# Gate and value of a SwiGLU feed-forward as block products of four by four blocks, 26 for 28 Strassen products, on one Trainium2 core

## Chip, cores, metric

One core of a Trainium2 chip (trn2), fp32 throughout. The time is the device time of one execution in microseconds (us), lowest is best. Before: 3118.09 us, the median of 4 runs (3117.6 to 3118.33) beside the changed kernel.

Engines in the profile: PE is TensorE's matmuls, PEld its weight loads, DVE is VectorE, ACT ScalarE, POOL GpSimd, SP the engine that only issues transfers here. L516 is line 516 of the kernel that is named.

## What is computed

```python
def _attn_ref(x, filt_r, filt_i):          # x: 8 x 3008 x 256
    X = np.fft.rfft(x, axis=1)
    Y = X * (filt_r + 1j * filt_i)[None, :, :]
    return np.fft.irfft(Y, n=x.shape[1], axis=1).astype(np.float32)

def _moe_ref(x, w_gate, w_val, w_out):      # x: 24064 tokens x 256; d_ff = 1536
    g = x @ w_gate
    silu = g * (1.0 / (1.0 + np.exp(-g)))
    return (silu * (x @ w_val) @ w_out).astype(np.float32)
```

The Fourier part is done by matmuls too (pa, pb, pc, pd in the profile). For each of 8 batches the feed-forward runs over 4 chunks of 752 tokens, while TensorE also does the Fourier part of the next batch in between. So there are 32 chunks, and the stretch of one batch is four of them.

## The kernel before

Gate and value are each a 2 x 2 block Strassen product with 7 products of 376 columns, for 6 slices of d_ff: 84 products a chunk. Twice a chunk, after three slices, the hidden values are projected back, with 7 products again (63 matmul pairs of 128 columns each time).

```python
    def hidden(b, k, j, y, fill):
        ...
            nc.tensor.matmul(out=bk[z][kind], lhsT=wt[z][:, j, LEFT[p], :], rhs=y[:, RIGHT[p], :],
                             start=start, stop=True, skip_group_check=True)
        ...  # banks are evicted by ScalarE (copies to u) and VectorE (u + bank)
        e = nc.gpsimd                      # Strassen sums of the hidden block for the projection
        add(e, h[:, 4], h[:, 1], h[:, 2])
        sub(e, h[:, 5], h[:, 0], h[:, 1])
        sub(e, h[:, 1], h[:, 4], h[:, 0])
        sub(e, h[:, 6], h[:, 3], h[:, 1])

    def project(b, k, q):
        ...
        def place(i, cb, a, kind):
            dst = o[i][:, :, ts(cb, 128)]
            if q:                          # not the first projection of the chunk
                add(nc.gpsimd, dst, dst, u[a])
                add(nc.vector, dst, dst, bk[kind])
            else:
                add(nc.vector, dst, u[a], bk[kind])
        ...
        product(7, "A", False)
        nc.scalar.copy(out=u[2], in_=bk["A"])
        place(1, 1, 2, "E")                # reads bank E ...
        product(4, "F4")
        place(1, 0, 2, "F4")
        product(3, "E", False)             # ... and this adds onto bank E
        place(0, 1, 1, "E")
```

`place(1, 1, 2, "E")` must have read bank E before the last product may add onto it.

Of the kernel before, what the change touches and what calls it, by code (L numbers as in the profile page):

```python
# [55 lines left out]
NQB = 2  # L57
JB = NJ // NQB

# [5 lines left out]

LEFT = {1: 0, 2: 1, 7: 2, 4: 3, 5: 4, 6: 5, 3: 6}
RIGHT = {1: 0, 2: 1, 3: 2, 4: 3, 5: 4, 6: 5, 7: 6}
WO = {1: 0, 7: 1, 2: 2, 3: 3, 5: 4, 6: 5, 4: 6}
HID = {1: 0, 6: 1, 4: 2, 2: 3, 5: 4, 7: 5, 3: 6}

# [33 lines left out]
def kernel(  # L104
# [30 lines left out]
    ypool = pool("yp", 2)  # L135
    dpool = pool("dram", 2, DRAM)
    fps = pool("fps", 2, PSUM)
    wps = pool("wps", 2, PSUM)
# [3 lines left out]
    wg_t = cpool.tile([128, NJ, 7, 128], FP32)  # L142
    wv_t = cpool.tile([128, NJ, 7, 128], FP32)
# [25 lines left out]
    def weight_parts():  # L169

        cols = [w.bitcast(U32).rearrange("(a p) (h j f two) -> j p h a f two",
                                         a=2, p=128, h=2, j=NJ, two=2)
                for w in (moe_w_gate, moe_w_val)]
        rows = moe_w_out.bitcast(U32).rearrange("(l j p) (c f two) -> j p l c f two",
                                                l=2, j=NJ, p=128, c=2, two=2)
        def hid(j):
            for w, dst in zip(cols, (wg_t, wv_t)):
                yield w[j], dst[:, j], True

        for q in range(NQB):  # L180
            for j in range(JB * q, JB * q + JB):
                yield from hid(j)
            for j in range(JB * q, JB * q + JB):
                yield rows[j], wo_t[:, j], False

    weights = list(weight_parts())
    raws = {}

    def load_weights(j, queue=nc.sync):
        if j < len(weights):  # L190
            raws[j] = rpool.tile([128, 2, 2, 128, 2], U32, name=f"raw_{j}", tag="raw", bufs=2)
            for i in range(2):
                ins = queue.dma_start(out=raws[j][:, i], in_=weights[j][0][:, i])
                if j in (2, 3):
                    tc.keep_in_program_order(ins)

    def round_weights(j, following=True):



        if following:
            load_weights(j + 2)
        raw, (_, dst, left) = raws.pop(j), weights[j]
        low, high = raw[:, :, :, :, 0], raw[:, :, :, :, 1]
        pw = rpool.tile([128, 2, 2, 128], U32, name=f"pw_{j}", tag="pw")
        w = rpool.tile([128, 2, 2, 128], FP32, name=f"w_{j}", tag="w")
        man = w.bitcast(U32)
        v = nc.vector
        flat = "p a b f -> p (a b f)"
        flat2 = "p a b f two -> p (a b f) two"  # L210
# [7 lines left out]
        pin(nc.scalar.activation(out=pw, in_=pw, func=AF.Relu, bias=off_t))  # L218
        v.tensor_scalar(out=pw, in0=pw, scalar1=255.0, scalar2=2.0 ** 23,
# [6 lines left out]
                               op0=ALU.mult, op1=ALU.add)  # L226

        e = nc.gpsimd
        pin(e.tensor_tensor(out=dst[:, 0:4, :].rearrange("p (a b) f -> p a b f", b=2), in0=w,  # L229
                            in1=pw.bitcast(FP32), op=ALU.mult))  # L230
        if left:
            a11, a12, a21, a22, s1, s2, s4 = [dst[:, i] for i in range(7)]
            add(e, s1, a21, a22)
            sub(e, s2, s1, a11)
            sub(e, a21, a11, a21)
            sub(e, s4, a12, s2)
        else:
            b11, b12, b21, b22, t1, t2, t4 = [dst[:, i] for i in range(7)]
            sub(e, t1, b12, b11)
            sub(e, t2, b22, t1)  # L240
            sub(e, b12, b22, b12)
            sub(e, t4, b21, t2)
# [3 lines left out]
    def bank(kind, name):  # L246
        return wps.tile([128, 512], FP32, name=f"w{kind}_{name}", tag=kind)

    def warm(count, width=4):


        for i in range(count):
            ps = bank("F", "idle")[:, 0:128 * width]
            tc.keep_in_program_order(nc.tensor.matmul(
                out=ps, lhsT=wv_t[:, 0, 0, :],
                rhs=wv_t[:, 0, 0:width, :].rearrange("p i f -> p (i f)"), start=True, stop=True))

    class Spectral:
# [81 lines left out]
        def stage2a(self, u):  # L340
# [6 lines left out]
            if self.b:  # L347
                ps = fps.tile([128, NV, C], FP32, name=f"pb_{self.b}_{u}", tag="f")
                ppool, qpool = apool, bpool
            else:  # L350

                ps = bank("AEF"[u % 3], f"b_{u}").rearrange("p (i c) -> p i c", i=NV)
                ppool = apool if u % 3 == 2 else spool0
                qpool = bpool if u % 2 else spool0
# [32 lines left out]
        def stage3(self, k, step):  # L387

            if step == 0:
                self.y[k] = ypool.tile([128, 7, TH], FP32, name=f"y_{self.b}_{k}", tag="y")  # L390
            y = self.y[k]
# [8 lines left out]
            def turned(p):  # L400
                return y[:, RIGHT[p], :].rearrange("p (r n) -> p n r", n=NH)

            def block(p):
                return y[:, RIGHT[p], :]

            if step == 0:
                nc.scalar.copy(out=turned(1), in_=psv)
            elif step == 1:
                nc.scalar.copy(out=turned(3), in_=psv)
            elif step == 2:  # L410
                sub(nc.vector, turned(5), psv, turned(1))
                sub(nc.vector, turned(7), turned(3), psv)
                sub(nc.gpsimd, block(6), block(3), block(5))
            else:
                nc.scalar.copy(out=turned(2), in_=psv)
                sub(nc.gpsimd, block(4), block(2), block(6))
# [5 lines left out]
    def hidden(b, k, j, y, fill):  # L422

        name = f"{b}_{k}_{j}"
        s = spool.tile([128, 4, TH], FP32, name=f"s_{name}", tag="s")
        h = hpool.tile([128, 7, TH], FP32, name=f"h_{name}", tag="h")
        dst = {"g": s, "v": h}
        wt = {"g": wg_t, "v": wv_t}
        bk = {"g": {}, "v": {}}
        ut = {}  # L430

        def product(z, p, kind, start=True):
            if start:
                bk[z][kind] = bank(kind, f"{z}{p}_{name}")[:, 0:TH]
            nc.tensor.matmul(out=bk[z][kind], lhsT=wt[z][:, j, LEFT[p], :], rhs=y[:, RIGHT[p], :],  # L435
                             start=start, stop=True, skip_group_check=True)

        def step(z, p):
            if p == 1:
                ut[z] = upool.tile([128, 3, 384], FP32, name=f"u_{z}_{name}", tag="u")  # L440
            u = [ut[z][:, i, 0:TH] for i in range(3)]
            if p in (1, 6, 7):
                product(z, p, "A", p == 1)
                nc.scalar.copy(out=u[(1, 6, 7).index(p)], in_=bk[z]["A"])  # L444
                if p == 7:
                    add(nc.vector, dst[z][:, 2], u[2], bk[z]["E"])
            elif p == 5:
                product(z, p, "E")
            elif p == 2:
                product(z, p, "F")  # L450
                add(nc.vector, dst[z][:, 0], u[0], bk[z]["F"])
            elif p == 4:
                product(z, p, "A", False)
                if z == "g":
                    nc.scalar.activation(out=s[:, 3], in_=bk[z]["A"], func=AF.Silu)
                else:
                    nc.vector.tensor_tensor(out=h[:, 3], in0=s[:, 3], in1=bk[z]["A"], op=ALU.mult)  # L457
            else:
                product(z, p, "E", False)
                add(nc.vector, dst[z][:, 1], u[1], bk[z]["E"])  # L460
                if z == "g":
                    nc.scalar.activation(out=s[:, 0:3], in_=s[:, 0:3], func=AF.Silu)  # L462
                else:
                    nc.vector.tensor_tensor(out=h[:, 0:3], in0=s[:, 0:3], in1=h[:, 0:3],  # L464
                                            op=ALU.mult)

        for it in ("g1", "v1", "g5", "v5", "g6", "v6", "", "g2", "g7", "v7", "v2", "",
                   "g4", "v4", "g3", "v3"):
            if it:
                step(it[0], int(it[1]))  # L470
            else:
                fill()

        e = nc.gpsimd
        add(e, h[:, 4], h[:, 1], h[:, 2])
        sub(e, h[:, 5], h[:, 0], h[:, 1])
        sub(e, h[:, 1], h[:, 4], h[:, 0])
        sub(e, h[:, 6], h[:, 3], h[:, 1])
        hids[b, k, j] = h

    def project(b, k, q):

        hs = [hids.pop((b, k, JB * q + i)) for i in range(JB)]
# [9 lines left out]
        def product(p, kind, start=True):  # L493
            if start:
                bk[kind] = bank(kind[0], f"o{p}_{name}")[:, 0:384].rearrange(
# [30 lines left out]
        if q == NQB - 1:  # L526
# [11 lines left out]
    todo = list(range(len(weights)))  # L538
# [3 lines left out]
    x0 = [wo_f[0:NR, 0:8 * C], wo_f[0:NR, 8 * C:16 * C]]  # L542
# [119 lines left out]
```

## Time and profile before

| | before |
|---|---|
| time | 3118 us |
| TensorE busy, granted clock | 98%, 0.99 |
| VectorE, GpSimd busy | 47%, 45% |
| one steady batch (4 chunks) | 376.2 us |
| of it matmul work | 373.7 us |

The ends of matmuls are modelled, their starts are not; so I took the start-to-start spacing of every matmul record and looked up what it is when nothing waits: 112 ns for one of 94 or 128 columns, 216 for 256, 316 for 376, 429 for 512 (each fp32 product is two such instructions). The sum of these is "work". What a spacing has above it is "half clock" as far as the clock records show half speed there, and "wait" otherwise. Over the whole run before: 3013.6 work, 15.9 half clock, 78.9 waits. The profile's lines on this kernel stand in the prediction.

### The profile page before, as it was taken

The numbers are of one execution on the slowest core, as the hardware profiler recorded it, in microseconds if no ns is written. First come the engines' busy times: TensorE is split into PE (matmuls) and PEld (weight loads), VectorE is DVE, ScalarE is ACT, GpSimd is POOL, SyncE is SP. The second block draws the span as 40 slices with busy tenths as digits, with TensorE's granted clock in tenths as the row PEclk, the third lists the DMA queues.
The fourth block names the chain that finished last, engine by engine and source line by source line (L and its number), as shares of the span: only waits on it lengthen the run. The fifth ranks groups of instructions, "written<-read, shape, count | busy, mean of one in ns | idle before, by whom it ended". The sixth has DMA issues, their size and how long they took to land.

```text
span 3116.7 us, 41163 instructions
## 1 busy us (share of the span) xinstructions
PE 3056.4 (98%) x15560; PEld 2240.5 (72%) x15560; DVE 1476.5 (47%) x2348; ACT 1140.3 (37%) x2070; POOL 1405.8 (45%) x1622
## 2 busy tenths in 40 slices
PE   7789999999999999999999999999999999999999
PEld 4457777777767777767777777767777677777776
DVE  4664553354543554345543455434553444544443
ACT  0443333333343343343333333343333433333333
POOL 3574454444543444444543454434544344533343
PEclk8999999999999999999999999999999999999999
DMA  8432222222212222222222132121322222200000
GB/s 233 130 117 68 72 81 56 61 76 68 75 55 72 59 79 60 61 68 81 69 60 65 57 88 71 51 71 55 91 68 56 63 63 68 68 28 21 21 6 16
DMA packets 123634, 212.51 MB, mean 68 GB/s; under 512 B 23670, under 2 KB 69750, under 8 KB 122578
## 3 DMA queue, kind: packets, MB, share of 16 engines
q1 hardware_dynamic: 91692, 132.25, 14.8%
q0 software_dynamic: 24448, 68.71, 7.7%
q10 hardware_dynamic: 7296, 8.92, 1.1%
q8 instruction: 123, 2.02, 0.3%
q14 instruction: 75, 0.61, 0.1%
HBM read 134.81 MB, written 74.97 MB: 67 GB/s over the span
## 4 chain that ended last, share of the span: by engine, by line
PE 80%; POOL 7%; DVE 6%; issue 3%; DMA 2%; ACT 2%; SPq 0%; POOLq 0%; ACTq 0%; DVEq 0%
PE wA_v L435 15%; PE wA_g L435 15%; PE wA_o L499 7%; PE wE_v L435 7%; PE wE_g L435 7%; PE wE_o L499 7%; PE wF_o L499 4%; PE wF_g L435 4%; PE pd L396 3%; PE wF_v L435 3%; POOL o L162 3%; PE pa L332 3%; POOL h L165 3%; PE pc L376 2%; PE pb L356 2%
## 5 line engine op out<-in xcount | busy, mean ns | idle before, releaser
L435 PE MATMUL wA_v<-y,wv_t 128*128 128x376 f32 x1536 | 612.5, 480 | 7.3 <-ACT u_v L444 4.3
L435 PE MATMUL wA_g<-y,wg_t 128*128 128x376 f32 x1536 | 614.3, 481 | 4.4 <-POOL wg_t L229 3.5
L165 POOL TENSOR_TENSOR h<-h 128x376 f32<-128x376 f32 x576 | 566.9, 984 | 28.8
L162 POOL TENSOR_TENSOR h<-h 128x376 f32<-128x376 f32 x192 | 188.4, 981 | 701.2 <-PE wE_v L435 389.1
L444 ACT COPY u_g<-wA_g 128x376 f32<-128x376 f32 x576 | 269.5, 468 | 589.9 <-PE wA_g L435 587.6
L435 PEld LDWEIGHTS wA_v<-y,wv_t 128*128 128x128 f32 x1536 | 289.2, 190 | 204.0 <-DVE h L457 15.6
L499 PEld LDWEIGHTS wA_o<-wo_t,h 128*128 128x128 f32 x3456 | 406.3, 192 | 16.3
L499 PE MATMUL wA_o<-wo_t,h 128*128 128x128 f32 x3456 | 417.5, 275 | 0.0
L435 PEld LDWEIGHTS wA_g<-y,wg_t 128*128 128x128 f32 x1536 | 281.1, 190 | 172.3 <-issue 28.1
L462 ACT ACTIVATE s<-s 128x1128 f32<-128x1128 f32 x192 | 219.5, 1143 | 373.2 <-DVE s L162 373.2
L464 DVE TENSOR_TENSOR h<-s,h 128x1128 f32<-128x1128 f32 x192 | 257.1, 1339 | 124.0 <-ACT s L462 124.0
L435 PE MATMUL wE_g<-y,wg_t 128*128 128x376 f32 x768 | 307.1, 482 | 2.1 <-DVE s L162 2.1
L435 PE MATMUL wE_v<-y,wv_t 128*128 128x376 f32 x768 | 306.1, 480 | 1.8 <-DVE h L162 1.6
L444 ACT COPY u_v<-wA_v 128x376 f32<-128x376 f32 x576 | 272.2, 473 | 69.3 <-PE wA_v L435 65.2
L162 DVE TENSOR_TENSOR s<-u_g,wE_g 128x376 f32<-128x376 f32 x384 | 208.9, 544 | 176.2 <-ACT u_g L444 174.6
L162 DVE TENSOR_TENSOR s<-u_g,wF_g 128x376 f32<-128x376 f32 x192 | 104.4, 544 | 394.9 <-PE wF_g L435 369.3
L499 PE MATMUL wE_o<-wo_t,h 128*128 128x128 f32 x2304 | 281.6, 276 | 7.5 <-DVE o L162 7.5
L499 PE MATMUL wF_o<-wo_t,h 128*128 128x128 f32 x2304 | 278.5, 275 | 0.0
L499 PEld LDWEIGHTS wE_o<-wo_t,h 128*128 128x128 f32 x2304 | 267.4, 192 | 13.6 <-DVE o L162 13.6
L499 PEld LDWEIGHTS wF_o<-wo_t,h 128*128 128x128 f32 x2304 | 267.8, 192 | 0.3
L162 POOL TENSOR_TENSOR p<-p,q 128x512 f32<-128x512 f32 x96 | 121.6, 1266 | 226.4 <-DVE q L367 226.4
L162 DVE TENSOR_TENSOR h<-u_v,wE_v 128x376 f32<-128x376 f32 x384 | 208.9, 544 | 26.5 <-ACT u_v L444 5.1
(86 smaller groups left out, 3275.3 us busy)
## 6 DMA issues: line engine op xcount, KB each, us to landing
t<-d SPq DMA_DIRECT2D x192, 128.0 KB
t<-d SPq DMA_DIRECT2D x64, 384.0 KB
d<-t POOLq DMA_DIRECT2D x112, 192.0 KB, 2.5
tb<-de_tbl SPq DMA_DIRECT2D x84, 256.0 KB
d<-g POOLq DMA_DIRECT2D x168, 128.0 KB, 2.8
x<-in_x_dram SPq DMA_DIRECT2D x112, 160.0 KB
out_dram<-o POOLq DMA_DIRECT2D x128, 128.0 KB, 2.0
f<-in_filt_r_dram SPq DMA_DIRECT2D x168, 64.0 KB
```

The source lines that it names most:

```text
L162: eng.tensor_tensor(out=dst, in0=a, in1=b, op=ALU.add)
L165: eng.tensor_tensor(out=dst, in0=a, in1=b, op=ALU.subtract)
L332: nc.tensor.matmul(out=ps[0:NK], lhsT=wf_t, rhs=self.x.pop(u), start=True, stop=True)
L356: nc.tensor.matmul(out=ps[:, i, :], lhsT=self.tb[u][:, i, 0, :], rhs=t2[:, i, :], start=True, stop=True)
L376: nc.tensor.matmul(out=ps[:, i, :], lhsT=tb[:, i, 1, :], rhs=pt[:, i, :], start=True, stop=True)
L396: nc.tensor.matmul(out=psv[:, n, :], lhsT=self.t4[k, i][:, n, ts(cb, 128)], rhs=wi_t, start=True, stop=True)
L435: nc.tensor.matmul(out=bk[z][kind], lhsT=wt[z][:, j, LEFT[p], :], rhs=y[:, RIGHT[p], :], start=start, stop=True, skip_group_check=True)
L444: nc.scalar.copy(out=u[(1, 6, 7).index(p)], in_=bk[z]["A"])
L462: nc.scalar.activation(out=s[:, 0:3], in_=s[:, 0:3], func=AF.Silu)
L464: nc.vector.tensor_tensor(out=h[:, 0:3], in0=s[:, 0:3], in1=h[:, 0:3], op=ALU.mult)
L499: nc.tensor.matmul(out=bk[kind][:, t, :], lhsT=hs[i][:, HID[p], t0:t0 + 128], rhs=wo_t[:, JB * q + i, WO[p], :], start=start and t == 0 an ...
```

## The change

The intent is to take matmul work off TensorE. The left operand is cut into groups of four blocks of 128 rows (two slices of d_ff, three groups a chunk), the sequence into four columns of blocks of 188 tokens, and one group's 4 x 2 by 2 x 4 block product takes 26 products where Strassen takes 28 and the plain form 32. Gate and value share their sequence operands and a bank. In exchange there are more sums: of the weights (26 a group, built once, kept in DRAM and loaded again for every group), of the sequence (26 tiles in y_t, once a chunk) and of the products. The projection comes three times a chunk with 42 matmul pairs.

```diff
-NQB = 2
-JB = NJ // NQB
+NG = 3
+JB = NJ // NG
+TQ = TH // 2
+ORDER = ("Q0 Q1 P0 P1 A01 Q2 E01 P2 B01 A02 A12 Q3 E02 B02 P3 E12 B12 "
+         "A03 A13 A23 E03 B03 E13 B13 E23 B23").split()
...
-    wps = pool("wps", 2, PSUM)
+    wps = pool("wps", 6, PSUM)
...
+    def reload_weights(g, piece):
+        a, b, _ = PIECES[piece]
+        nc.sync.dma_start(out=wt_t[:, a:b], in_=w_dram[g, :, a:b])
...
+        def sums(i, j):
+            r = rpool2.tile([128, 3, 2, TQ], FP32, name=f"r{i}{j}_{name}", tag="r")
+            rt[i, j] = [r[:, e] for e in range(3)]
+            add(nc.gpsimd, rt[i, j][0], qp[i][0], qp[j][1])
+            add(nc.vector, rt[i, j][1], qp[j][0], qp[i][1])
...
+            elif kind == "A":
+                sums(i, j)
+                nc.scalar.copy(out=rt[i, j][2], in_=ps)
+                add(nc.gpsimd if j == 2 else nc.vector, rt[i, j][1], rt[i, j][1], rt[i, j][2])
+            elif kind == "B":
+                sub(nc.vector, place(i, j), ps, rt[i, j][0])
+            else:
+                sub(nc.vector, place(j, i), ps, rt[i, j][1])
+            if p in ("B13", "B23"):
+                h = hs[p == "B23"]
+                nc.scalar.activation(out=h[:, 4:8], in_=h[:, 4:8], func=AF.Silu)
+                nc.vector.tensor_tensor(out=h[:, 0:4], in0=h[:, 0:4], in1=h[:, 4:8], op=ALU.mult)
+                e = nc.gpsimd
+                add(e, h[:, 4], h[:, 1], h[:, 2])
+                ...                        # three more; eight a group
...
             hidden(b, k, g, fill, after)
+            if k < NCHUNK - 1 and g == NG - 1:
+                combine_sequence(cur.y[k + 1])
             if late is not None:
                 project(*late)
```

## The prediction

> **What bounds the kernel now.** I read the page's busy shares first, then the groups with each shape kept apart, then the timeline of two projections, then the chain of waits through one of them.
>
> ```profile
> PE 3056.4 (98%) x15560; PEld 2240.5 (72%) x15560; DVE 1476.5 (47%) x2348; ACT 1140.3 (37%) x2070; POOL 1405.8 (45%) x1622
> ```
>
> TensorE is busy 98%, every other compute engine under half. But the ends of matmuls are modelled, so I take their cost from start to start:
>
> ```profile
> 1510.69 2.17 PE L499 MATMUL wF_o<-wo_t,h 128*128 128x128 f32 x18
> 1512.70 2.17 PE L499 MATMUL wE_o<-wo_t,h 128*128 128x128 f32 x18
> 1514.71 0.80 PE L435 MATMUL wA_g<-y,wg_t 128*128 128x376 f32 x2
> 1515.34 0.79 PE L435 MATMUL wA_v<-y,wv_t 128*128 128x376 f32 x2
> 1515.97 0.80 PE L435 MATMUL wE_g<-y,wg_t 128*128 128x376 f32 x2
> ```
>
> Each fp32 product is two instructions. Nine products of 128 columns start 2.01 us apart: 0.223 us each. One of 376 columns takes 0.63. Weight loads are hidden in both. One chunk (376 tokens per half, all of d_ff) recurs every 94.05 us: the first projection of a chunk starts at 1124.45 and, four chunks later, at 1500.64. Of this 84 hidden products make 53.2 us (84 x 0.633), 126 projection products 28.1, the spectral work of the next batch 12. So it is truly TensorE-bound, except at one place, the second projection of a chunk:
>
> ```profile
> 2017.18 1.33 DVE L464 TENSOR_TENSOR h<-s,h 128x1128 f32<-128x1128 f32 x1 [0.58 <-ACT s L462]
> ...
> 2018.66 0.98 POOL L162 TENSOR_TENSOR h<-h 128x376 f32<-128x376 f32 x1 [3.73 <-DVE h L464]
> 2019.60 0.98 POOL L165 TENSOR_TENSOR h<-h 128x376 f32<-128x376 f32 x1
> ...
> 2020.53 1.00 POOL L162 TENSOR_TENSOR o<-o,u 128x384 f32<-128x384 f32 x1
> 2021.49 2.04 POOL L165 TENSOR_TENSOR h<-h 128x376 f32<-128x376 f32 x2
> ...
> 2026.66 1.95 POOL L162 TENSOR_TENSOR o<-o,u 128x384 f32<-128x384 f32 x2 [2.18 <-ACT u L520]
> 2027.68 0.56 DVE L162 TENSOR_TENSOR o<-o,wE_o 128x384 f32<-128x384 f32 x1 [2.97 <-POOL o L162]
> ...
> 2028.29 1.94 PE L499 MATMUL wE_o<-wo_t,h 128*128 128x128 f32 x15 [0.22 <-DVE o L162]
> ```
>
> Here the last projection product adds onto a bank that VectorE must first read; VectorE first needs GpSimd's add into o; and GpSimd works off, in order, the sums of the hidden block that has just ended. TensorE waits 0.4 us only. This chain decides my prediction.
>
> **What the Trainium skill says.** "SBUF — State Buffer", Who interferes with whom: a VectorE operation with two SBUF inputs and a GpSimd operation that reads SBUF exclude each other for the whole instruction; with one input in PSUM there is no conflict. The trace agrees:
>
> ```profile
> L365 DVE SCALAR_TENSOR_TENSOR q<-pb,f 64x512 f32<-64x512 f32 x84 | 58.2, 693 | 1.1
> ...
> L224 DVE SCALAR_TENSOR_TENSOR w<-raw,w 128x512 f32<-128x512 uint32 x18 | 15.4, 853 | 1.3 <-ACT w L215 0.8
> ```
>
> Same width; the second has both inputs in SBUF while GpSimd works, and its mean is 160 ns longer. "VectorE: DVE Perf Modes", The TRN2 errata: an fp32 tensor_tensor takes (N+151)/0.96 ns; 1128 columns give 1332, measured 1339. "Perfetto Trace Analysis", Per-engine timelines: time GpSimd by start-to-start spacing. Above that is 0.94 to 0.96 us for 376 columns. "TensorE: Matmul & The Clock Gate", Part 1: an idle window of some 3.4 us halves the clock until a busy window has passed. In the start-up the trace shows it after gaps shorter than that, with the same four matmuls:
>
> ```profile
> 81.13 1.13 PE L376 MATMUL pc<-p,tb 128*128 128x256 f32 x4 [1.69 <-POOL p L162]
> 83.96 2.08 PE L376 MATMUL pc<-p,tb 128*128 128x256 f32 x4 [1.70 <-POOL p L162]
> ```
>
> **The change, part by part.**
>
> *TensorE.* A chunk has three groups, each of 26 products for gate and for value on 188 columns: 156 products for 84. Between 128 columns (0.223) and 376 (0.633) a column costs 1.65 ns, so 188 take 0.322. 156 x 0.322 = 50.3 us, 2.9 less per chunk; over 32 chunks 93 us, 3.0%. A projection now has 42 products (9.4 us) for 63 (14.1), three times a chunk instead of twice: the same 28.1.
>
> *VectorE, ScalarE, GpSimd.* Per group, VectorE has 26 operations of 376 columns (0.46 start to start: 12.0) and two products of 1504 (1.72 each), together 15.4 us against some 10 for two hidden blocks before. GpSimd has 16 of 0.96, 15.4 us against 7.7. Per chunk VectorE also builds the sequence sums (about 5 us), and four more evictions. I get some 67 us of VectorE (65 to 73) and 66 to 70 of GpSimd in 92 us of TensorE. Neither is above TensorE, so the sum of busy times does not decide. ScalarE stays under half.
>
> *The chain.* Put T where the last product of a hidden block ends. VectorE takes it off PSUM by T+0.7. Silu of the second half tile (1504 columns; by the 1143 ns for 1128 an estimate of 1.46) ends at T+2.3. VectorE's products run from T+0.9 and from T+2.5 to T+4.1; the second keeps GpSimd out, so GpSimd's first sum ends at about T+5.0. The instruction order of the changed kernel then puts, ahead of the first add that the last projection product needs, all eight sums of the hidden block and two or three adds into o.
> - Third projection of a chunk: ten more operations at 0.96 and a DMA issue, T+15.1, VectorE's read 0.6: T+15.7. TensorE has until then 36 products (8.0), one spectral matmul (0.9) and half a new product (0.3): T+9.2. It stands 6.5 us.
> - Second projection: the new chunk's sequence sums come between. GpSimd nine at 0.96, one of 1.27, one of 564 columns (1.4); VectorE's early spectral operation 0.7, and its sums with two SBUF inputs hold GpSimd off for about 2.5. T+20.1. TensorE has work up to T+11.8. It stands 8.3 us.
> - First projection: nothing is added into o, no wait.
>
> Together 14.8 us per chunk, for 0.4 now. Both gaps exceed a clock window; I charge 2 us each for matmuls at half clock afterwards: 4.
>
> *Weights.* 3.4 MB are loaded per group, some 320 MB in all, 110 GB/s on top of 68. The start-up reaches 331 GB/s in one 10 us window. Each piece is asked for as soon as its slots are read and has 15 us or more: hidden.
>
> *Start.* The second and third group's weights are rounded and combined during the first two groups, on VectorE and GpSimd, which are then the bound: an estimate of +25 us.
>
> *Sum.* Per chunk -2.9 - 0.4 + 14.8 + 4 = +15.5; times 32 is 496; the last batch, with no spectral operations between, stands about 12 less in all; the start +25. 3118 + 496 - 12 + 25 = 3627, say 3620.
>
> **The rivals.**
> 1. *TensorE's arithmetic wins.* The sums and adds are hidden and 93 us are gained: 3025 to 3050. For it: all engines keep under 80%. Against: this chain already binds by 0.4 us with four sums, 14.1 us of projection and no lock; now there are eight and 9.4. Even without any lock GpSimd's eleven operations end at T+13, 4 us late.
> 2. *The shared port or VectorE binds all over.* In a group the operations that exclude each other hold the port for some 26 of 30 us. Waits would then lie on the hidden products (for banks VectorE has not read), not on the projection's last. Alone 3250 to 3450; on top of my chain 3750 and more.
> 3. *Late weights.* Waits of hidden products on the DMA at the 1st, 8th, 15th or 21st product; every us late costs 96 us. Against: 15 us of slack for some 5 us of transfer.
> 4. *The chain without the clock.* If gaps don't lower the clock, 3620 - 128 = 3490.
>
> **Range and chances.** The least that the order allows (no lock, no clock loss) is about 4 us a wait, 8 a chunk: 3118 + 32 x 5 + 25, about 3300. Rival 2 on top gives the far end. I take 3420 to 3780 for eight in ten. Faster by over 2% needs the chain to be wrong altogether: 0.04; within 2%: 0.03; slower: 0.93.
>
> **What would show it.** Right: hidden products start 0.32 us apart when nothing waits; in TensorE's waits the projection (L578) stands for VectorE's o some 400 to 500 us in total, 64 times, 5 to 9 us each; GpSimd's h and o carry a third or more of the chain that ended last; the granted clock falls from 0.99 to about 0.94; GpSimd and VectorE are at 55 to 65%; HBM reads grow by some 320 MB with hardly a wait on wt_t. Wrong: if the waits lie on the hidden products (L516), it is rival 2; on the DMA, rival 3; if the projection's wait is under 2 us, GpSimd's sums are earlier than I place them and rival 1 holds.

## The result, and the profile after

Slower, as predicted, but by more: 3919.51 us, the median of 4 runs (3917.47 to 3925.16), 1.257 times before (95% interval 1.255 to 1.260). This and every ratio below is the mean time of one kernel's fast runs over that of the other's of the same rounds, so not quite the ratio of the medians. Two kernels were run only once.

The page of the changed kernel, busy shares and the granted clock in 40 slices:

```profile
PE 3185.0 (81%) x20114; PEld 2974.8 (76%) x20114; DVE 2773.3 (71%) x4050; ACT 1285.9 (33%) x2298; POOL 2498.3 (64%) x2522
...
PEclk9768999998899999999999999999889999888999
```

TensorE is no longer busy nearly all the time, and its clock drops again and again. The waits of the changed kernel (engine and line, what it waited for, us in total, times, longest):

```profile
PE wo L578 <- DVE o L181: 512.0, 64, 10.4
DVE o L181 <- POOL o L181: 459.2, 152, 9.2
```

These are the two links that the prediction names: 64 waits, two a chunk, 8.0 us each in the mean (63 of 6.7 to 10.4 us, and one of 0.9 in the last projection of all). One of them, a second projection (start, duration, instruction, in brackets the idle time before it and its releaser), to be held against the timeline in the prediction:

```profile
1008.45 3.34 DVE L548 TENSOR_TENSOR h<-h 128x1504 f32<-128x1504 f32 x2
...
1009.92 2.73 POOL L181 TENSOR_TENSOR o<-o,u 128x384 f32<-128x384 f32 x1 [4.23 <-ACT u L592]
...
1012.61 0.99 POOL L181 TENSOR_TENSOR h<-h 128x376 f32<-128x376 f32 x1
1013.55 3.68 POOL L184 TENSOR_TENSOR h<-h 128x376 f32<-128x376 f32 x3
1013.95 3.88 DVE L181 TENSOR_TENSOR y_t<-y_t 128x564 f32<-128x564 f32 x3
...
1017.20 1.48 POOL L181 TENSOR_TENSOR h<-h 128x376 f32<-128x376 f32 x1
...
1018.64 1.28 POOL L184 TENSOR_TENSOR h<-h 128x376 f32<-128x376 f32 x1
1019.88 1.29 POOL L181 TENSOR_TENSOR o<-o,u 128x384 f32<-128x384 f32 x1
...
1021.14 2.14 POOL L184 TENSOR_TENSOR h<-h 128x376 f32<-128x376 f32 x2
...
1025.90 1.94 POOL L181 TENSOR_TENSOR o<-o,u 128x384 f32<-128x384 f32 x2
1026.92 0.55 DVE L181 TENSOR_TENSOR o<-o,wo 128x384 f32<-128x384 f32 x1 [3.43 <-POOL o L181]
...
1027.53 2.93 PE L578 MATMUL wo<-wo_t,h 128*128 128x128 f32 x12 [8.94 <-DVE o L181]
```

GpSimd's first add into o takes 2.73 us, for 0.98 where VectorE stands idle beside it (at 824.78), while VectorE runs its two products of h. Then GpSimd works through the sums of h in its order, held up a little by VectorE's sums of y_t, and only then comes to the add into o that lets the bank be read. The last product of the hidden block ended at 1005.99; TensorE goes on at 1027.53.

The same by stretches. Columns: from and to, length, then busy time and instruction count of PE, PEld, DVE, ACT, POOL, then granted clock, DMA share, GB/s. First the kernel before: first batch, a steady one, the last:

```profile
104.92:500.55 395.63, 374.23 (x1834) 266.12 (x1835) 224.44 (x356) 158.98 (x287) 218.00 (x248) 0.98 0.29 86
1252.91:1629.10 376.19, 375.19 (x1937) 277.54 (x1936) 175.72 (x281) 140.97 (x256) 169.60 (x196) 1.00 0.24 67
2757.65:3116.66 359.01, 351.40 (x1903) 265.54 (x1901) 147.72 (x237) 124.21 (x229) 139.42 (x156) 1.00 0.05 16
```

The changed kernel, the same three:

```profile
112.42:666.82 554.40, 408.68 (x2414) 375.53 (x2412) 412.40 (x672) 182.51 (x341) 348.70 (x386) 0.85 0.44 141
1596.05:2062.73 466.68, 391.01 (x2514) 370.02 (x2513) 337.15 (x477) 158.16 (x280) 305.52 (x305) 0.92 0.45 142
3456.33:3918.13 461.80, 366.10 (x2450) 355.12 (x2448) 289.13 (x432) 138.62 (x249) 285.65 (x270) 0.91 0.29 94
```

By spacings, the whole run is now 2880.9 work (132.7 less: 116.3 in the hidden products, 16.4 in warm-up products that the change drops), 172.3 half clock (156.4 more) and 849.5 waits (770.6 more), of which 631 stand before projection matmuls. Six steady batches took a mean of 464.9 us each, 88.7 more than before; the first 158.8 more, the last 102.8 more, the start-up before the first 7.5 more: 6 x 88.7 + 158.8 + 102.8 + 7.5 = 801.

### The profile page after: what moved, and what is told of

Same layout as the page of the kernel before. It is cut to its first block, busy times and chain, and to the rows that moved or that the text cites. A ratio compares the mean times of both kernels' runs of the same rounds, so it can differ in the third digit from the quotient of the medians.

```text
span 3918.1 us, 55923 instructions
## 1 busy us (share of the span) xinstructions
PE 3185.0 (81%) x20114; PEld 2974.8 (76%) x20114; DVE 2773.3 (71%) x4050; ACT 1285.9 (33%) x2298; POOL 2498.3 (64%) x2522
## 4 chain that ended last, share of the span: by engine, by line
PE 43%; POOL 19%; DVE 14%; issue 9%; ACT 7%; DMA 1%; DVEq 0%; POOLq 0%; ACTq 0%; SPq 0%
PE wQ L516 12%; PE wA L516 11%; PE wo L578 11%; POOL h L184 9%; ACT h L547 6%; DVE h L184 5%; PE wE L516 5%; DVE r L181 5%; POOL o L181 4%; POOL h L181 4%; PE pd L462 2%; PE pa L399 1%; POOL p L181 1%; PE pc L443 1%; DVE h L548 1%
## 5 line engine op out<-in xcount | busy, mean ns | idle before, releaser
L578 PE MATMUL wo<-wo_t,h 128*128 128x128 f32 x8064 | 1053.2, 292 | 577.8 <-DVE o L181 512.0
L578 PEld LDWEIGHTS wo<-wo_t,h 128*128 128x128 f32 x8064 | 1010.7, 205 | 635.5 <-DVE o L181 530.6
L181 POOL TENSOR_TENSOR r<-q,q 128x376 f32<-128x376 f32 x576 | 641.6, 1126 | 581.4 <-DVE q L184 289.9
L516 PE MATMUL wA<-y_t,wt_t 128*128 128x188 f32 x4608 | 886.7, 328 | 30.1 <-ACT r L539 24.4
L516 PEld LDWEIGHTS wA<-y_t,wt_t 128*128 128x128 f32 x4608 | 769.3, 193 | 78.1 <-ACT r L539 44.1
L516 PE MATMUL wQ<-y_t,wt_t 128*128 128x188 f32 x3072 | 658.0, 352 | 34.4 <-POOL wt_t L272 26.4
L516 PEld LDWEIGHTS wQ<-y_t,wt_t 128*128 128x128 f32 x3072 | 560.7, 211 | 71.7 <-POOL wt_t L272 31.3
L181 DVE TENSOR_TENSOR r<-q,q 128x376 f32<-128x376 f32 x576 | 566.9, 990 | 35.8 <-ACT q L533 15.5
L516 PE MATMUL wE<-y_t,wt_t 128*128 128x188 f32 x2304 | 467.0, 326 | 3.1 <-DVE h L184 3.1
L516 PEld LDWEIGHTS wE<-y_t,wt_t 128*128 128x128 f32 x2304 | 390.4, 193 | 3.4 <-DVE h L184 3.4
```

Source lines behind the costliest of these rows:

```text
L181: eng.tensor_tensor(out=dst, in0=a, in1=b, op=ALU.add)
L516: nc.tensor.matmul(out=bk[key][:, z], lhsT=wt_t[:, SLOT[p], z], rhs=y_t[:, RHS[p]], start=start and z == 0, stop=True, skip_group_check=True)
L578: nc.tensor.matmul(out=bk[kind][:, t, :], lhsT=hs[i][:, HID[p], t0:t0 + 128], rhs=wo_t[:, JB * q + i, WO[p], :], start=start and t == 0 an ...
```

## Experiments

Eleven kernels ran beside the changed one. The first table gives time and what one steady batch is made of (by spacings, us). "wo" are waits before the projection, "hidden" before the hidden products, "pc" before a Fourier stage. Before: 376.2, of it work 373.7, waits 2.5.

| kernel | time | to before | steady batch | half clock | wo | hidden | pc |
|---|---|---|---|---|---|---|---|
| changed | 3919.5 | 1.257 | 464.9 | 17.7 | 74 | 6 | 7 |
| swap | 3635.8 | 1.165 | 427.8 | 12 | 20 | 29 | 7 |
| warm_wait | 3896.7 | 1.249 | 461.8 | 6 | 28 | 7 | 7 |
| no_reload | 3915.4 | one look | | | | | |
| no_prep | 3847.0 | one look | 465 | 18 | 74 | 6 | 7 |
| swap_psum | 3635.7 | 1.166 | 430.0 | 15.5 | 15 | 35 | 5 |
| swap_dve | 3531.4 | 1.132 | 417.0 | 10 | 20.5 | 16 | 10 |
| relief | 3417.5 | 1.096 | 402.8 | 5.6 | 3.6 | 30 | 4.7 |
| relief_early | 3371.7 | 1.081 | 397.4 | 4.4 | 6.2 | 23.5 | 4.4 |
| no_hsums | 3414.9 | 1.095 | 402.8 | 5.5 | 24 | 7 | 7 |
| no_sums | 3249.2 | 1.042 | 385.7 | 4.4 | 15 | 3 | 4 |
| bare | 3108.1 | 0.997 | 375.0 | 0 | 8 | 3 | 4 |

Work is 359.2 in every row of the changed form, save warm_wait (414.1, its needless products). no_reload, no_prep, no_hsums, no_sums and bare give a wrong result.

### swap: the two adds into o exchanged

```diff
             if q:
-                add(nc.gpsimd, dst, dst, u[a])
                 add(nc.vector, dst, dst, bk[kind])
+                add(nc.gpsimd, dst, dst, u[a])
```

> Only the order of the two adds into o is exchanged (VectorE's read of the bank first, GpSimd's add of u after it), so GpSimd's queue no longer stands between VectorE's read and the last projection product. Theory (the projection's last product waits for VectorE, which waits for GpSimd's o add behind eight h sums): the waits of the projection's matmuls on VectorE's o fall from 512 us to under 130 us (what VectorE's own queue of sequence sums leaves in the second projection), the half-clock time falls with them, some 18 us per chunk are saved, total 3300 to 3400. Rival A (VectorE or the shared port binds by itself): the waits only move, to the hidden products or to the next use of GpSimd's results, total above 3700. Rival B (DMA of weights): no change, 3900.

Measured: 3635.8 us (3631.65 to 3636.63), ratio 1.165 (1.163 to 1.167). The result is correct. 284 us came back with one exchanged pair of lines, so the chain is shown; but I expected twice that. Per batch the waits before the projection fell by 54 us, half clock by 6, and 23 came back before the hidden products. The waits of this kernel:

```profile
PE wQ L516 <- ACT q L533: 134.6, 62, 6.5
PE wo L578 <- DVE o L181: 101.0, 18, 6.2
```

And one such wait on a hidden product, in its timeline:

```profile
1435.36 1.31 POOL L181 TENSOR_TENSOR o<-o,u 128x384 f32<-128x384 f32 x1
...
1439.05 2.35 POOL L610 DMA_DIRECT2D out_dram<-o  x4
...
1441.42 0.99 POOL L181 TENSOR_TENSOR r<-q,q 128x376 f32<-128x376 f32 x1
...
1442.44 0.55 DVE L184 TENSOR_TENSOR h<-wA,r 128x376 f32<-128x376 f32 x1 [5.72 <-POOL r L181]
...
1443.10 0.47 ACT L539 COPY r<-wA 128x376 f32<-128x376 f32 x1 [5.50 <-DVE h L184]
1443.47 0.48 ACT L533 COPY q<-wQ 128x376 f32<-128x376 f32 x1
...
1444.00 1.30 PE L516 MATMUL wQ<-y_t,wt_t 128*128 128x188 f32 x4 [3.75 <-ACT q L533]
```

Read it from below: TensorE wants a bank that ScalarE has not copied out; ScalarE stands in its own order behind a copy into r, whose buffer VectorE has not read; VectorE waits for GpSimd's r; GpSimd comes to it only after the sums of h, the adds into o and the output's transfers. The late GpSimd had been hidden by TensorE's longer wait before. Rival A of this run is right for that part: the wait moved.

### warm_wait: TensorE kept busy while it waits

```diff
+        if q:
+            idle = fps.tile([128, 512], FP32, name=f"idle_{name}", tag="f")
+            for _ in range(8):
+                tc.keep_in_program_order(nc.tensor.matmul(
+                    out=idle, lhsT=wo_t[:, 0, 0, :],
+                    rhs=wo_t[:, 0, 0:4].rearrange("p i f -> p (i f)"), start=True, stop=True))
         product(3, "E", False)
```

> Eight needless 512-column products (about 0.86 us each at full clock, 6.9 us) are put right before the last projection product when it must wait; result unchanged. Theory (some 170 us of the loss are matmuls at half clock after those waits): the granted clock rises from 0.91 to 0.95 or more, total about 100 us less (3820), though the waits on VectorE's o are as long as before, seen from the end of the product before. Rival (gaps don't matter for the clock, or the loss has another cause): the same or up to 100 us more, since the needless work sticks out past the wait in some places, 3920 to 4020.

Measured: 3896.7 us (3894.79 to 3897.67), 23 us less than the changed kernel, not 100. The clock did what was expected, here in one steady batch:

```profile
1600.00:2061.00 461.00, 431.49 (x2640) 378.50 (x2639) 337.72 (x477) 158.18 (x280) 306.62 (x305) 0.99 0.46 144
```

By spacings over the run, half clock fell from 172.3 to 80.8, so 91.5 us of the loss were the clock's. But the 439.3 us of needless work replaced only 369.7 us of waits. 439.3 - 369.7 - 91.5 = -21.9: the needless products stick out where the wait was shorter than they are. The clock loss is shown; as a remedy it isn't worth much.

### no_reload: the weights stay as they are in SBUF

```diff
-                    if n == end and not last and (b or step > 1):
+                    if False:
                         reload_weights((g + 1) % NG, piece)
```

> The weights are never loaded again from DRAM after the first chunk (wrong result on purpose), some 320 MB of reads fewer. Theory (transfers are hidden): within 1% of the changed kernel, 3880 to 3940. Rival (weights' transfers or their contention cost several us a chunk): 3600 to 3800.

Measured, one look, wrong result: 3915.4 us. HBM reads before the edit and after it:

```profile
HBM read 451.75 MB, written 85.20 MB: 137 GB/s over the span
```

```profile
HBM read 134.81 MB, written 85.20 MB: 56 GB/s over the span
```

317 MB fewer, and 4 us less than the changed kernel's median: 2 us below the fastest of its runs, which lie 8 us apart. The transfers are hidden, as far as one look can tell.

### no_prep: the second and third group's weights not prepared

```diff
-        for g in range(NG):
-            for i in range(4):
-                if (g, i) == (NG - 1, 3):
-                    yield from proj(0)
-                yield from hid(g, i)
-        for j in range(1, NJ):
+        for i in range(4):
+            yield from hid(0, i)
+        for j in range(NJ):
...
-    hid = {4: "rr", 6: "rr", 8: "rr", 9: [(0, 1), 0], 15: "rr", 17: [(0, 2), (1, 2), 1],
-           25: [(0, 3), (1, 3), (2, 3), 2, 3]}
+    hid = {9: [0], 17: [1], 25: [2, 3]}
```

> The weights of the second and third group are not rounded and combined; the first group's sums are stored three times (wrong result on purpose). Theory (the preparation on VectorE and GpSimd during the first two groups costs some 75 us over a steady batch): the first batch falls from 554 us to 480 to 500, total 3840 to 3870, the other batches stay at 465. Rival (the first batch is slow for another reason, for instance the clock or the spectral work of the next batch): under 20 us saved.

Measured, one look, wrong result: 3847.0 us. Its first batch:

```profile
111.50:594.60 483.10, 389.05 (x2414) 362.52 (x2413) 368.37 (x562) 168.13 (x309) 317.49 (x326) 0.91 0.47 153
```

483.1 for 554.4: the preparation costs 71 us, all in the first batch. The other batches are as they were. In the waits view of the first batch, TensorE waits 31.0 us for GpSimd's rounding of wo_t and 26.4 for wt_t in the changed kernel, and 4.5 and 9.1 here.

### swap_psum, swap_dve, relief, relief_early: what binds after the exchange

All four keep the exchange and give correct results. swap_psum takes the A product into r from PSUM, without a copy:

```diff
-                nc.scalar.copy(out=rt[i, j][2], in_=ps)
-                add(nc.gpsimd if j == 2 else nc.vector, rt[i, j][1], rt[i, j][1], rt[i, j][2])
+                add(nc.vector, rt[i, j][1], rt[i, j][1], ps)
```

> On top of the swapped adds, the 18 sums a chunk that add the A product to r take it straight from PSUM (VectorE, one input in PSUM) instead of from ScalarE's copy in SBUF; GpSimd loses its 6 of them. Theory (after the swap, GpSimd's queue and the port it shares with VectorE are what binds: by my count from the durations about 67 us of GpSimd and 29 us of two-SBUF-input VectorE work a chunk exclude each other, 96 us for 90 of TensorE): about 11 us of exclusive time leaves the chunk, waits fall by 4 to 8 us a chunk, total 3380 to 3520. Rival (TensorE waits for the order of queues alone, not for the port's load): within 1% of the swap, 3600 to 3660.

Measured: 3635.7 us (3631.87 to 3641.32), no gain at all. My count of exclusive port time as a bound is wrong: GpSimd's busy time in a steady batch fell by 26 us (308.2 to 282.5) and the time didn't follow. The edit does show what two inputs in SBUF cost: VectorE's add of A to r took a mean of 723 ns in swap, with both in SBUF, and 535 ns here, with one in PSUM. The wait only changed its place, since the A bank is now released by VectorE, in VectorE's order:

```profile
PE wA L516 <- DVE r L181: 180.2, 145, 6.3
```

swap_dve gives the add of u to VectorE as well:

```diff
                 add(nc.vector, dst, dst, bk[kind])
-                add(nc.gpsimd, dst, dst, u[a])
+                add(nc.vector, dst, dst, u[a])
```

> On top of the swapped adds, the add of u into o is VectorE's too (0.47 for GpSimd's 0.96 us, 8 a chunk), nothing else. Theory (port and GpSimd's queue bind): GpSimd gets to the next group's first r sum 4 us earlier in two of three groups and the port is free for 4 us more a chunk; 3520 to 3600. Rival (VectorE, busiest with 76%, is the bound now): slower than the swap, 3650 to 3750.

Measured: 3531.4 us (3527.6 to 3534.36), inside the theory's range, though it makes VectorE, the busier of the two, busier still. That speaks for it that at this point what counts is when GpSimd gets to the next group's sums, and not VectorE's load. GpSimd's load falls here too (by 29 us a batch), so this run alone doesn't separate its order from its load; swap_psum, where nearly as much fell away without gain, speaks for the order.

relief is both, and moves transfers off GpSimd's queue:

```diff
-                    nc.gpsimd.dma_start(           # the output
+                    nc.sync.dma_start(
...
-            queue = nc.scalar if self.b == 1 else nc.gpsimd    # stores of the first stage
+            queue = nc.scalar if self.b else nc.gpsimd
...
-                queue = nc.gpsimd if self.b else nc.scalar     # stores of the second stage
+                queue = nc.scalar
```

> All three: swapped adds, A products added from PSUM, u added by VectorE, and besides GpSimd's DMA issues (0.6 us each, 6 for the output and 5 for the spectral stores a chunk) given to the idle queues of SP and ScalarE. Exclusive port time by my count 81 us a chunk for 90 of TensorE. Theory: waits of the hidden products nearly vanish, what is left is the second projection's wait behind the sequence sums (5 us a chunk) and the start-up; 3280 to 3400. Rival (VectorE binds, or ScalarE's queue is held up by the issues): 3450 or more.

Measured: 3417.5 us (3415.52 to 3420.15), a little above the theory's range. Here the waits before the projection nearly went (3.6 us a batch), but waits on hidden products stayed at 30 us. Part of these is the old wait in another place: the longest, 4.4 us twice in the steady batch from 1429.61, are wQ products for a bank of the second projection that VectorE reads only after its sequence sums (72.6 us in 21 waits of wQ on VectorE's o in the run).

relief_early also makes the new chunk's sequence sums earlier, in three parts:

```diff
+                if g == NG - 1 and k < NCHUNK - 1 and n in (15, 23):
+                    combine_sequence(cur.y[k + 1], "a" if n == 15 else "b")
...
-                combine_sequence(cur.y[k + 1])
+                combine_sequence(cur.y[k + 1], "c")
```

> As the last, and three of four times the new chunk's sequence sums are made during the hidden group before, as soon as the products that read the old ones are through, in place of between hidden group and projection. Theory: of the second projection's wait (some 5 us a chunk) most goes; 100 us less than without it, 3180 to 3300. Rival (the sums only delay VectorE's evictions earlier): no gain or a loss against it.

Measured: 3371.7 us (3371.22 to 3375.57), 46 us less than relief, half of what I expected. It is the fastest form with a correct result, and 8.1% slower than before. One steady batch:

```profile
1404.66:1801.34 396.68, 376.62 (x2515) 351.49 (x2513) 341.99 (x533) 127.48 (x208) 216.44 (x185) 0.99 0.53 167
```

VectorE is busy 342 of 397 us, time behind the lock included (the exclusion of VectorE and GpSimd that the prediction describes). Each repair left a smaller wait somewhere else.

### no_hsums, no_sums, bare: is the saving on TensorE there at all?

no_hsums drops GpSimd's eight sums after each hidden block and leaves the adds into o in the change's order:

```diff
-                add(e, h[:, 4], h[:, 1], h[:, 2])
-                sub(e, h[:, 5], h[:, 0], h[:, 1])
-                sub(e, h[:, 1], h[:, 4], h[:, 0])
-                sub(e, h[:, 6], h[:, 3], h[:, 1])
```

> The changed kernel without GpSimd's eight sums at the end of each hidden block (wrong result on purpose); the order of the adds into o is as in the change. Theory (these eight, 7.7 us, are what makes VectorE's read late, and GpSimd's load is what the exchanged order only shifted to the next group): the projection's waits on VectorE's o fall from 512 us to under 60, and the waits do not reappear on the hidden products as they did after the exchange; total 3200 to 3350. Rival (VectorE is what binds, GpSimd only seems to): as after the exchange, 3550 to 3650.

Measured, wrong result: 3414.9 us (3411.55 to 3417.13). The waits on o fell, and nothing reappeared on the hidden products (7 us a batch for the 29 of swap); that part of the theory holds, and the rival's range is missed. But the waits on o are twice what I allowed:

```profile
PE wo L574 <- DVE o L181: 117.9, 64, 4.4
DVE o L181 <- POOL o L181: 98.1, 84, 2.8
```

So dropping the eight sums takes away 512 - 118 = 394 of the 512 us. What is left, 1.8 us a wait, must come from what still stands in the chain (the silu, the product, the sequence sums and the adds into o), which I had taken to fit before TensorE is ready; the shares were not separated.

no_sums drops the sums into r as well, and ScalarE's copy of A:

```diff
-            add(nc.gpsimd, rt[i, j][0], qp[i][0], qp[j][1])
-            add(nc.vector, rt[i, j][1], qp[j][0], qp[i][1])
+            rt[i, j] = [qp[i][1], qp[j][0]]
...
-                nc.scalar.copy(out=rt[i, j][2], in_=ps)
-                add(nc.gpsimd if j == 2 else nc.vector, rt[i, j][1], rt[i, j][1], rt[i, j][2])
```

> As the last, and also without all sums into r on GpSimd and VectorE and ScalarE's copy of A (wrong result on purpose); TensorE's work is untouched. Theory (TensorE's saving of some 116 us in the hidden products is real and only covered): steady batches near 370 us with 359 of matmul work, total 3050 to 3130, what remains being the start-up. Rival (the halved products cost TensorE something in themselves, bank changes or the reload of weights): 3200 or more.

Measured, wrong result: 3249.2 us (3247.53 to 3251.1): the rival's number. But the rival's cause is not there: matmul work by spacings is 2880.9 us as in the changed kernel, and hardly a hidden product waits. What is left is named by the waits:

```profile
PE wo L569 <- DVE o L181: 87.3, 64, 3.5
```

The long ones are all in the second projection, but not with one cause. In the steady batch from 1345.70, one of 3.5 us stands behind VectorE's sequence sums. Two of 2.5 us stand behind GpSimd: its adds into o come after its add for the Fourier part, which waits for VectorE's Fourier products behind the two products of h. The fourth is 0.6 us. The first batch still takes 462.6 us.

bare drops these two as well: the sequence sums are made once, and the weights are not prepared as in no_prep.

```diff
-            if k < NCHUNK - 1 and g == NG - 1:
-                combine_sequence(cur.y[k + 1])
-            elif g == NG - 1 and b < B - 1:
-                combine_sequence(spec.y[0])
```

> As the last (no h sums, no r sums), and also the sequence sums made only once and the weights of the second and third group not prepared (wrong result on purpose); all of TensorE's products stay. Theory (the 26 products of 188 columns cost TensorE less than the 28 of before, and everything above that is side work in TensorE's way): steady batches 360 to 366 us for 376.2 before, first batch 380 to 410, total 2990 to 3070, faster than before by 2 to 4%. Rival (something that the products themselves bring, such as twice as many banks to free or the reload of the weights, takes the saving): 3118 or more.

Measured, wrong result: 3108.1 us (3106.56 to 3111.25), ratio 0.997 (0.995 to 0.9985). I expected 2990 to 3070. A steady batch:

```profile
1250.04:1625.62 375.58, 366.75 (x2515) 348.92 (x2514) 203.06 (x312) 124.43 (x200) 90.67 (x109) 1.00 0.56 177
```

Work is 359.2, 14.5 less than before, as it should be. 15.7 us of waits are left, the longer ones of 0.7 to 1.6 us, half of them before a projection (on VectorE's o, 0.6 to 0.8 us each in the waits view) and the rest before a Fourier stage and single hidden products. Before had 2.5. So even with nearly all its side work taken away the change breaks even, no more, in this order of instructions.

## Why the prediction was wrong in size

The direction, the mechanism and the place were right, the size was not: 801 us on the profiled runs for a predicted 509 (3627 - 3118), outside the range. The step that failed is the sum. Its +15.5 per chunk counted two waits and the clock, and took every other wait of TensorE as nothing; measured was +22.2, which makes 213 of the missing 292 us. Its "+25" for the start was 78 (start-up and first batch, less four chunks), and its "12 less" in the last batch was 14 more, which makes 53 and 26. Term by term, by batches (predicted, measured; "start-up and first batch" holds the first batch's four chunks):

| term | predicted | measured |
|---|---|---|
| six steady batches | 24 x 15.5 = 372 | 532 |
| last batch | 62 - 12 = 50 | 103 |
| start-up and first batch | 62 + 25 = 87 | 166 |
| sum | 509 | 801 |

**The steady chunk**, +15.5 predicted, 88.7 / 4 = +22.2 measured. Its terms:

- TensorE's products: -2.9 predicted, -3.6 measured. The interpolated 0.322 us for a product of 188 columns was 0.317. Right.
- The two waits of the chain: 14.8 predicted; on the page 512 / 32 = 16.0. The mechanism is right (swap takes it away, no_hsums takes 394 of the 512 away). In a steady batch the second projection waits a mean of 8.4 us for the 8.3 of the prediction, the third 7.7 for 6.5. What was late is the beginning. I let GpSimd's first sum of h end at T+5.0. It ended at T+7.6 in the second projection shown (T is 1005.99) and at T+6.3 in a third one (819.63, where T is 813.34), since the first silu began only at T+0.6 and VectorE's two products of h ended at T+5.8 and T+5.5 for the T+4.1 of the prediction (in the second projection GpSimd's first add into o came first as well). From that first sum to the add that releases the bank, GpSimd took 13.3 us for 14.5 predicted in the second projection, and 9.9 for 10.1 in the third. So what I allowed for the lock behind the sequence sums was enough. TensorE in turn had work for 0.6 to 0.8 us longer than I counted.
- Other waits before the projection: left out. They were another 2.6 a chunk (74.4 / 4 = 18.6, less 16.0), short waits for the bank that ScalarE copies to u (32.6 us in 80 waits in the run), and what the spacings show as wait and the waits view, which goes by modelled ends, does not.
- Half clock: 4 predicted, 17.7 / 4 = 4.4 measured, and warm_wait takes half of it away in all. Right, and rival 4 (no effect of gaps on the clock) falls.
- Waits elsewhere, on pc, A and Q: 0 predicted, 3.4 measured (13.6 a batch). Rival 2 said this would be so if the port or VectorE bound, and I left it out of the sum. It is a small part of the changed kernel. Once the chain is cut it grows to 9 a chunk (swap), so the chain had been hiding it.

Sum: -3.6 + 16.0 + 2.6 + 4.4 + 3.4, less the 0.6 of waits of before, is 22.2. The two terms for waits that I didn't have, 2.6 and 3.4, and the 1.2 of the chain make the miss here.

**The last batch**: I said that, with no spectral operations in between, it stands 12 us less, since GpSimd's queue is shorter. This step failed: it stands more, 90.3 us before the projection for 74.4. By spacings, the eight long waits that it shares with a steady batch sum to 65.5 us for 66.0, so the shorter queue brought nothing. It also holds a ninth, of 7.5 us: the second projection of the last chunk, a place whose wait in other batches falls behind the next batch's first product (the first batch holds only six of the chain's waits). And the short waits for ScalarE's u are 10.3 us for 2.6 in the waits view. Why these grew was not looked into.

**The start**: "an estimate of +25 us" for the preparation. no_prep shows 71 in the first batch. The estimate named the right engines, but it was made without a count of their instructions or of TensorE's waits for weights that are not ready (31.0 and 26.4 us, above).

**What held**: hidden products 0.32 us apart, 64 waits on VectorE's o (512 us for "400 to 500"), no gain from leaving out the reload of the weights (no_reload), no wait of the chain at the first projection of a chunk. The lock holds too, though the two lines shown in the prediction differ in more than their inputs. Taken one by one, L224's instructions in the kernel before took 679 to 692 ns where no GpSimd operation ran beside them (3), and 757 to 1469 in 14 of the other 15.

**What did not**: the granted clock is 0.91 for "about 0.94". GpSimd's h and o carry 17% of the chain that ended last (h 9% and 4%, o 4% on the page) for "a third or more". VectorE is busier than said (71% for 55 to 65%, with GpSimd at 64%); part of that is time behind the lock, which counts as busy.

**What stays open**: the exclusive port was my theory for what binds after the exchange, and swap_psum speaks against it as a budget. Which part of the last 30 us of waits in relief_early is the lock and which the order of the queues was not separated. And whether an order exists that gets a correct version under 3118 us is open; bare makes it unlikely without also cutting the short waits before the projections.

## What to carry to other kernels

Here the engines beside TensorE were under half busy, and still the order of their work decided the time. Before counting what is saved on TensorE, follow the longest in-order queue that stands between the last read of a bank (a piece of PSUM) and its next use. An add that only has to happen some time (here o += u) must not stand ahead of one that frees a bank, and exchanging two lines was worth 284 us. But a wait that is taken away uncovers the next; run the change once with all its side work removed, because that says what it can bring in its present order of instructions: here 0.3%, where the matmul work alone is less by 132.7 us, 4.3%.

## What the Trainium skill lacked or had wrong

- "TensorE: Matmul & The Clock Gate", Part 1, says that after at least one idle window of some 3.4 us the clock is halved. For long waits it holds here: each of the changed kernel's 61 gaps of 7 to 9 us between matmuls set off a record of half clock, two or three times 3.41 us long. But gaps shorter than a window do it too: 13 of 25 gaps of 2.4 to 3.0 us in no_sums did. In seven batches of it the gap at one place did every time and the gap at another, of the same 2.66 us, never, so the length alone doesn't decide. None of 39 gaps of 1 to 1.8 us that met a full clock in the changed kernel did. (In the start-up of before, three gaps of 1.7 us in a row were enough.) The page speaks of frequent short idles as a cause, but has no figure for such gaps.
- The same page, Back-to-back issue gap, gives spacings without saying for which type, and none for fp32. In fp32 a product is two instructions here, each 158.5 ns apart at 188 columns, 316 at 376, 429 at 512, twice what the formula gives (81, 159, 216), and 112 at both 94 and 128 columns.
- "SBUF — State Buffer", Who interferes with whom, has the lock right, and has no figure for what it costs in a stream of mixed work. Here VectorE's sums of two SBUF tiles of 376 columns (r from q) took a mean of 990 ns over 576 of them, for 0.54 us when alone. GpSimd's sums of the same kind took 1126 ns, for some 0.96 us when alone.
- No page says that time behind this lock is shown as busy time. The 990 ns for 540 above are such time, and VectorE's 71% in the changed kernel contains them, so a busy share is no measure of an engine's load here.
